# A planned attention-and-MLP kernel: load order, a third pair in halves, a new rule of choice in the planner, and one Gelu table load per phase

## The chip, the cores and the metric

The kernel runs on one core of a Trainium2 chip. The metric is the device time of one execution in microseconds, median of several runs. TensorE is called PE, VectorE DVE, ScalarE ACT, GpSimd POOL.

## The reference, cut to what matters

Inputs q, k, v and alpha are `(4, 8, 768, 48)`; the MLP is 384 -> 2048 -> 384.

```python
for t in range(S):                                     # gated linear attention, a state of 48 x 48 per head
    state = alpha[:, :, t, :, None] * state + einsum('bhd,bhe->bhde', k[:, :, t], v[:, :, t])
    y[:, :, t] = einsum('bhd,bhde->bhe', q[:, :, t], state)
x = y.transpose(0, 2, 1, 3).reshape(3072, 384)
h = x @ w_in
return gelu_tanh(h) @ w_out
```

## The kernel before

The 768 tokens are cut into 6 chunks of 128. A *unit* is one chunk of one batch, a *pair* is two units, and there are 12 pairs, 0 to 11. Each pair has a recurrent part (Ln of alpha, a cumulative sum as a matmul, exponentials, scaled q and k, their transposes, scores, mask, y, transposed x) and a *block* of MLP: layer 1 with 48 matmuls and 16 Gelus, layer 2 with 32 matmuls. Ln and Exp share one activation table, Gelu needs another, so ACT works in phases: the exponentials of the pair after next, then the Gelus of a block, then exponentials again.

The instruction order is not written by hand. A planner in the kernel knows every task with assumed durations and puts them in a fixed order. This is the choice that it makes for each engine:

```python
for t in left[e]:
    at = ready(t)
    if at is not None:
        found.append((max(at, free[e] + (W["table"] if t.table not in (None, table) else 0)), t))
if found:
    window = min(f[0] for f in found) + 60
    at, t = min((f for f in found if f[0] <= window), key=lambda f: (f[1].prio, f[0]))
```

`W["table"]` is 1290 ns. The copies (`x`, `ot`, and `ev` for the transposes of the first two pairs) can go to ACT or DVE and need no table. Other parts that matter:

```python
BUFS = dict(ca=1, yk=2, ff=4, ...)          # PSUM: "ca" single, for sums and scores; "ff" for hT and acc
LN_EXP, GELU = 6, 0
...
cum = s.add("cum", {"PE": W["cum"]}, P + 1, self.cum(u), [ln])        # P = 100 * pair; lower goes first
...
rows(0, 0, "qkv"); weights("in", (0, 1)); rows(0, 1); weights("in", (2, 3)); weights("out", range(4))
for c, i in pairs[2:]: rows(c, i)
...
for t in order:
    if t.load is not None:
        self.act_set(t.load)                # writes an ACT_TABLE_LOAD for Ln/Exp and for Gelu
    t.emit(t.engine)
```

## Time and profile before

| | before |
|---|---|
| median, four runs | 205.78 us (204.83 to 205.93) |
| profiled span | 204.1 us |
| PE busy / ACT busy / DVE busy | 185.2 / 151.0 / 105.6 us |
| table loads written / added at the Gelu | 20 / 10, each 1.283 us |
| mean granted clock of PE | 0.979 |

Busy time is a union over the span. The chain of the page follows the work that ended last backwards. A wait line reads "who waited, for whom: us in sum, times, longest". In a timeline, `[0.66 <-ACT gT L369]` is idle time just before the line and what ended it. In the names, `la` is Ln of alpha, `cum` its sum, `b`, `binv` and `bend` the exponentials, `qp` and `kp` the scaled q and k, `at` the scores, `yps` and `x` the result y and its copy, `hT` a layer-1 sum, `gT` its Gelu, `acc` and `ot` a layer-2 sum and its copy. The lines are in the prediction.

### The profile page before, as it was taken

What the parts mean: (1) busy time and instruction counts of PE and PEld (TensorE: products, weight loads), DVE (VectorE), ACT (ScalarE), POOL (GpSimd) and SP (SyncE); (2) the same over time, 40 slices, a digit from 0 to 9 for tenths busy, and PEclk for the clock granted to TensorE, in tenths of its full rate; (3) what the DMA queues carried; (4) which work ended last, traced back from release to release, by engine and by line L of the source; (5) the groups of instructions that cost most, each with busy time, mean ns of one, the idle gap of its engine ahead of it and who ended that gap; (6) DMA issues with size and microseconds to landing.
All of it is one profiled execution on the core that took longest, in us unless ns stands there. A gap on an engine that the chain in (4) does not pass through costs nothing.

```text
span 204.1 us, 4664 instructions
## 1 busy us (share of the span) xinstructions
PE 185.2 (91%) x1925; PEld 133.7 (65%) x1927; DVE 105.6 (52%) x219; ACT 151.0 (74%) x317; POOL 61.3 (30%) x63
## 2 busy tenths in 40 slices
PE   7786489999899989989989989989989989989992
PEld 2343358866578667767767767767777776676861
DVE  6373642037987394494494593594593550650000
ACT  2635767971789698798798798798798888883740
POOL 7983653464655664422410510000000000000000
PEclk9999958999999999999999999999999999999998
DMA  7999999999999999997980580200200200200202
GB/s 137 166 226 172 200 202 220 177 175 238 226 221 154 182 235 186 181 244 145 161 189 2 130 181 2 80 0 3 77 0 3 77 3 0 79 3 6 75 0 77
DMA packets 37941, 24.68 MB, mean 121 GB/s; under 512 B 27904, under 2 KB 34560, under 8 KB 37920
## 3 DMA queue, kind: packets, MB, share of 16 engines
q0 software_dynamic: 32400, 19.27, 67.2%
q1 hardware_dynamic: 5520, 5.11, 8.3%
q8 instruction: 15, 0.25, 0.6%
q14 instruction: 6, 0.05, 0.1%
HBM read 25.17 MB, written 4.72 MB: 146 GB/s over the span
## 4 chain that ended last, share of the span: by engine, by line
PE 70%; ACT 16%; DMA 6%; POOL 4%; issue 1%; DVE 1%; POOLq 0%; DVEq 0%
PE acc L377 31%; PE hT L363 27%; DMA k<-in_k_dram 6%; ACT L369 6%; ACT L181 6%; PE at L290 2%; PE yps L339 2%; ACT ot L384 2%; ACT gT L369 2%; PE cum L232 2%; PE yps L336 2%; PE xT_ps L353 2%; POOL q L202 1%; PE qkT_ps L268 1%; PE kv L307 1%
## 5 line engine op out<-in xcount | busy, mean ns | idle before, releaser
L363 PE MATMUL hT<-xT,w_in 128*128 128x256 bf16 x576 | 74.9, 278 | 8.1 <-ACT gT L369 7.9
L377 PE MATMUL acc<-w_out,gT 128*128 128x384 bf16 x384 | 68.4, 326 | 0.0
L369 ACT ACTIVATE gT<-hT 128x256 bf16<-128x256 f32 x192 | 62.0, 388 | 6.1 <-PE hT L363 5.6
L363 PEld LDWEIGHTS <-w_in 128*128 128x128 bf16 x576 | 54.6, 99 | 17.5 <-issue 9.4
L377 PEld LDWEIGHTS <-gT 128*128 128x128 bf16 x384 | 36.0, 98 | 20.4
L297 DVE TENSOR_TENSOR atm<-at,ut 128x512 bf16<-128x512 f32 x48 | 30.8, 684 | 8.1 <-PE at L290 7.0
L257 DVE TENSOR_TENSOR qp<-q,b 128x768 bf16<-128x768 f32 x12 | 11.5, 958 | 32.8 <-ACT b L249 32.8
L181 ACT ACT_TABLE_LOAD x20 | 25.7, 1283 | 1.1 <-PEq L576 0.7
L384 ACT COPY ot<-acc 128x384 f32<-128x384 f32 x18 | 8.6, 478 | 16.9 <-PE acc L377 16.7
L202 POOL DMA_DIRECT2D v<-in_v_dram x12 | 13.8, 1153 | 17.6 <-PE xT_ps L353 9.7
L346 ACT CAST x<-yps 128x384 bf16<-128x384 f32 x22 | 10.5, 478 | 11.5 <-PE yps L339 11.3
L202 POOL DMA_DIRECT2D a<-in_alpha_dram x11 | 12.7, 1153 | 20.7 <-ACT la L222 13.4
L278 DVE COPY qkT<-qkT_ps 128x1024 bf16<-128x1024 bf16 (+1 forms) x21 | 13.3, 673 | 7.6 <-PE qkT_ps L268 7.6
L357 DVE COPY xT<-xT_ps 128x384 bf16<-128x384 bf16 x24 | 8.5, 356 | 16.6 <-PE xT_ps L353 16.5
L202 POOL DMA_DIRECT2D q<-in_q_dram x12 | 14.0, 1163 | 9.9 <-DVE qp L257 4.2
L202 POOL DMA_DIRECT2D k<-in_k_dram x12 | 13.8, 1152 | 4.8 <-DVE stmp L322 2.3
L249 ACT ACTIVATE b<-cum 128x768 bf16<-128x768 f32 x12 | 9.7, 810 | 7.4 <-PE cum L234 7.4
L222 ACT ACTIVATE la<-a 128x768 f16<-128x768 f32 x12 | 10.1, 843 | 4.1 <-DMA a<-in_alpha_dram 4.0
L369 ACT ACT_TABLE_LOAD x10 | 12.8, 1283 | 0.1
L257 DVE TENSOR_TENSOR kp<-k,binv 128x768 bf16<-128x768 f32 (+1 forms) x14 | 11.6, 837 | 2.4 <-DMA k<-in_k_dram 2.4
L190 PE MATMUL idle<-zero 128*128 128x512 bf16 x37 | 11.3, 432 | 1.3 <-DVE zero L542 1.2
L324 DVE TENSOR_TENSOR st<-stmp,bend 64x192 bf16<-64x192 f32 x32 | 11.3, 353 | 1.7
(43 smaller groups left out, 167.2 us busy)
## 6 DMA issues: line engine op xcount, KB each, us to landing
q<-in_q_dram POOLq DMA_DIRECT2D x12, 384.0 KB, 12.6
k<-in_k_dram POOLq DMA_DIRECT2D x12, 384.0 KB, 12.7
out_dram<-ot SPq DMA_DIRECT2D x24, 192.0 KB, 1.9
a<-in_alpha_dram POOLq DMA_DIRECT2D x11, 384.0 KB, 12.6
v<-in_v_dram POOLq DMA_DIRECT2D x12, 192.0 KB, 12.6
w_in<-in_moe_w_in_dram POOLq DMA_DIRECT2D x4, 384.0 KB, 10.1
w_out<-in_moe_w_out_dram POOLq DMA_DIRECT2D x4, 384.0 KB, 14.7
a<-in_alpha_dram SPq DMA_DIRECT2D x1, 384.0 KB, 4.1
```

The lines of the kernel that those rows point to most:

```text
L181: nc.scalar.add_instruction(mybir.InstLoadActFuncSet(name=nc.get_next_instruction_name(), act_func_set_id=i, engine=mybir.EngineType.Activ ...
L190: self.nc.tensor.matmul(ps, self.zero[:, 0:self.C], self.zero, start=True, stop=True)
L202: (nc.sync if e == "SP" else nc.gpsimd).dma_start(t.rearrange("t b h d -> t (b h) d"), src)
L257: self.nc.vector.tensor_tensor(u[n + "p"][:, lo:hi, :, 0:self.D], u[n][:, lo:hi], u["b" if n == "q" else "binv"][:, lo:hi], op=ALU.mult)
L278: self.copy(e)(t, u.pop(("T_ps", i, which)))
L297: self.nc.vector.tensor_tensor(u["atm", i][:, o], u["at", i][:, o], self.ut[:, None, :].to_broadcast([self.C, self.H // 2, self.C]), op=AL ...
L324: nc.vector.tensor_tensor(new[ps, :, fs], acc, u["bend"][ps, i, :, None].to_broadcast([64, H // 2, D]), op=ALU.mult)
L346: self.copy(e)(x, u["y", i].rearrange("t h d -> t (h d)"))
L363: self.nc.tensor.matmul(h, self.w_in[:, j, nt * self.C:(nt + 1) * self.C], self.xT[c][:, j, lo:hi].rearrange("p g t -> p (g t)"), start=j ...
L369: return lambda e: self.nc.scalar.activation(self.gT[c % self.NG][:, nt, lo * self.C:hi * self.C], f.pop(("h", c, lo, nt)), AF.Gelu_apprx_ ...
L377: self.nc.tensor.matmul(f["acc", c, b], self.gT[c % self.NG][:, nt, b * self.C:(b + 1) * self.C], self.w_out[:, nt, :], start=nt == 0, sto ...
L384: self.copy(e)(f["ot", c, b], f.pop(("acc", c, b)))
```

## The change

Its intent: pairs 0 and 1 land first, then all weights, then the rest; pair 2 is loaded and scaled in halves; the cumulative sum is put ahead of other work; only the Ln/Exp table is loaded by hand. The diff also touches the planner's rule of choice and the idle matmuls that keep PE's clock up. Cut to its core:

```diff
+    SPLIT = (2,)
+    LOADS = ("0", "1", "in 0", "in 1", "in 2", "in 3", "out 0", "out 1", "out 2", "out 3", "2", "3", ...)
 ...
-                        found.append((max(at, free[e] + (W["table"] if t.table not in (None, table) else 0)), t))
+                        turn = W["table"] if t.table not in (None, table) else 0
+                        at = max(at, free[e] + turn)
+                        found.append((at, t, at - turn))
                 if found:
-                    window = min(f[0] for f in found) + 60
-                    at, t = min((f for f in found if f[0] <= window), key=lambda f: (f[1].prio, f[0]))
+                    window = min(f[2] for f in found) + 60
+                    at, t, _ = min((f for f in found if f[2] <= window), key=lambda f: (f[1].prio, f[0]))
 ...
                 n = int((at - max(free[e], ...) - 100) * 0.8 // W["fill"])
+                if not free[e]:
+                    n = int((at - W["zero"]) // W["cold"])
 ...
-            cum = s.add("cum", {"PE": W["cum"]}, P + 1, self.cum(u), [ln])
+            for lo, hi in self.parts(m):            # one part, or two where the pair is split
+                cum = s.add("cum", {"PE": W["cum"] * n // 2}, P - 400, self.cum(u, lo, hi), [ln])
 ...
-            if t.load is not None:
-                self.act_set(t.load)
+            if t.load == LN_EXP:
+                self.act_set(LN_EXP)
```

Cut: the bookkeeping for halves, a larger qkT tile, options that stay off (transposes by DMA), retuned durations, and a new order in layer 2 of block 0, which now takes each part of w_out for both units before the next part.

## The prediction

> **What bounds the kernel now.** I read the page first (busy shares, slices, chain), then the waits of PE, then the timeline in three places: one steady period, the start, and the passage to the third block. The work is 12 pairs of (chunk of 128 tokens, two batches), called pair 0 to 11. Each pair has a recurrent part and a block of layer 1 (48 matmuls and 16 Gelus, called L1) and layer 2 (32 matmuls, L2).
>
> ```profile
> PE 185.2 (91%) x1925; PEld 133.7 (65%) x1927; DVE 105.6 (52%) x219; ACT 151.0 (74%) x317; POOL 61.3 (30%) x63
> ...
> PE   7786489999899989989989989989989989989992
> ...
> PEclk9999958999999999999999999999999999999998
> DMA  7999999999999999997980580200200200200202
> ...
> PE 70%; ACT 16%; DMA 6%; POOL 4%; issue 1%; DVE 1%; POOLq 0%; DVEq 0%
> ```
>
> PE is busy 91% of the span and is 70% of the chain. Below 9 it dips in the first six slices, where the clock also drops to 5 tenths, and then once in every three slices. DMA is full until slice 18, about 92 us. So PE is the bound from about 57 us, and the start belongs to transfers and waits. All PE waits between 71 and 190 us, where PE is busy 113.05 of 118.9 us, are one group:
>
> ```profile
> PE hT L363 <- ACT gT L369: 5.8, 8, 0.9
> ```
>
> One period of the steady part shows what they are:
>
> ```profile
> 85.49 0.48 ACT L384 COPY ot<-acc 128x384 f32<-128x384 f32 x1 [0.39 <-PE acc L377]
> ...
> 85.98 1.28 ACT L181 ACT_TABLE_LOAD   x1
> ...
> 87.27 1.28 ACT L369 ACT_TABLE_LOAD   x1
> ...
> 88.57 2.50 ACT L369 ACTIVATE gT<-hT 128x256 bf16<-128x256 f32 x8
> 89.00 0.49 PE L363 MATMUL hT<-xT,w_in 128*128 128x256 bf16 x3 [0.66 <-ACT gT L369]
> ```
>
> Two table loads run back to back. The first (L181) is the one that the kernel writes; the second stands at the Gelu's own line and the kernel does not write it. PE has filled its four PSUM buffers of hT by then and stands 0.66 us for the first Gelu. The page counts 20 loads at L181 and 10 at L369: 10 for Ln/Exp, 10 written for Gelu, 10 more at the Gelu. The start shows the same pair of loads:
>
> ```profile
> 21.67 1.03 DVE L257 TENSOR_TENSOR kp<-k,binv 128x384 bf16<-128x384 f32 x2 [1.32 <-DMA k<-in_k_dram]
> 21.86 1.17 POOL L202 DMA_DIRECT2D a<-in_alpha_dram  x1 [1.81 <-DMA k<-in_k_dram]
> ...
> 23.33 1.28 ACT L181 ACT_TABLE_LOAD   x1
> ...
> 24.61 1.28 ACT L369 ACT_TABLE_LOAD   x1
> ...
> 26.34 0.80 PE L363 MATMUL hT<-xT,w_in 128*128 128x256 bf16 x3 [2.13 <-ACT gT L369]
> ```
>
> Here k of pair 1 lands at 21.67 us; its transposes are copied by ACT before the table is changed, so the first Gelu comes at 25.91. PE is empty from 24.4 to 26.34 and then has a clock of 0.57 until 32.8 (a window over that stretch). Blocks 0 and 1 end their L1 at 39.4. Last, the passage to block 2:
>
> ```profile
> 45.52 0.85 ACT L222 ACTIVATE la<-a 128x768 f16<-128x768 f32 x1
> ...
> 52.62 0.33 PE L232 MATMUL cum<-la,ut_h 128*128 128x384 f16 x1
> ...
> 57.89 0.66 ACT L369 ACTIVATE gT<-hT 128x256 bf16<-128x256 f32 x2
> ```
>
> The Ln of pair 3 is done at 46.4, but its cumulative sum waits to 52.62: the PSUM buffer "ca" is single, shared with the attention scores, and the two units of pair 2 are placed first. Gelu of block 2 needs the exponentials of pair 3, so it starts at 57.89, while L1 of block 2 starts at 57.14 behind 0.7 to 1 us of idle fill.
>
> **What the Trainium skill says.** "ScalarE: Activation LUTs", section "What ACT_TABLE_LOAD costs", gives about 1283 ns for a load plus a drain of about 1380. The trace agrees on 1283 and shows no drain here: 85.98, 87.27 and 88.57 follow one another with ACT already empty. The same page, "Table sets: the hidden batching unit", says that a compiler pass puts a load before every activation that needs one, and that the tanh-approximated Gelu is a set of its own. That fits a second load beside the written one; leaving out the written load should then be safe and cost nothing. "TensorE: Matmul & The Clock Gate", section "Part 1: The HAM clock gate", has half clock after an idle window of about 3.4 us. The trace shows about half clock (0.57), with 15 L1 matmuls in 3.20 us against 15 in 1.64 later; the empty stretch before was only 1.94 us, though there were others before it. "DMA: Bandwidth & Descriptors", section "Specifications", has rows under 512 B as slow. Agreed: a strip of q or k has rows of 192 B, and a 384 KB strip takes 2.35 us (q of pair 1 at 19.3, k at 21.67), a weight part of twice the bytes read about 1.9.
>
> **The change, part by part.** *Loads.* Bytes do not change, only their order: two weight parts pass behind pair 1. From the POOL waits (POOL waits for the transfer eight issues earlier) the landings before are: k of pair 0 9.3, second w_in part 15.05, alpha of pair 1 16.9, q 19.3, k 21.67, third and fourth w_in 24.7 and 26.4, w_out 28.4, 30.3, 32.4 and about 34.4, alpha of pair 2 36.45, alpha of pair 3 44.7. Moving 2 x 1.9 us of weights gives as estimates: alpha of pair 1 13.1, q 15.5, k 17.8, v 19.3; w_in 21.2, 23.1, 24.8, 26.4; w_out and pair 3 as before.
> Pair 1 then finishes its recurrent part near 24.5 instead of 33.5. L1 of block 0 starts with the first w_in at about 21.2 and is paced by the parts; its last four rows start at 26.4 and take 12 x 0.109 = 1.3 us, so it ends at 27.8. L1 of block 1 is 48 x 0.109 = 5.25 us, to 33.1. Before, that point was 39.4: 6.2 us gained, of which some 2.5 is the slow clock (30 matmuls at 0.21 instead of 0.109, less what lay beside), because PSUM is free for idle fill until 21.2.
>
> *Third pair unit by unit, cumulative sum first.* In halves, alpha of unit 0 lands near 35.5 and unit 1's k near 41.7. The "ca" buffer is free of pair 2's sums only after unit 1's exponentials, about 41.6. Attention of its units then takes the buffer to about 45.4 (twice a score group and 1.29 us of masks). Alpha of pair 3 lands at 44.7, Ln ends 45.5, its sum is now placed before other work, and its three exponentials end near 47.9; one table load gives a Gelu at about 49.2. PE has from 33.1 on: L2 of two blocks 64 x 0.163 = 10.4, pair 2's part 3.9 (the steady period's 14.37 busy less 5.25 and 5.21), pair 3's sum 0.5: to about 48.0. So L1 of block 2 starts effectively at 48.3 instead of 57.14: 8.8 us in all, including the 6.2.
>
> *One load per phase.* Ten loads of 1.283 us go, 12.8 us of ACT. PE gets back only its own waits: 5.8 us in eight phases. The first phase's share and block 2's are inside the 8.8. Layer 1, layer 2 and the tail after the last matmul (3.7 us) do not change. Splitting pair 2 adds some ten small instructions off the path.
>
> Sum: 204.1 - 8.8 - 5.8 = 189.5 us of span. I add 1.5 us for what a fixed order always loses against such arithmetic (parts of w_in that come late, PE waiting in order behind a half pair). That is 191.0; the timed runs lie 1.6 us over the profiled span (205.69 against 204.1), so 192.6, rounded to 192.5.
>
> **The rivals.** First: ACT stays the bound of the period. ACT's loop is Gelu start to last Gelu 5.9 us, then x copy, load, Ln, sum, exponentials, ot copy, two loads to the next Gelu start, about 9.1; that is 15.0, exactly the period. With one load it is 13.8, under PE's 14.37, so PE takes over with 0.6 us to spare. If other waits eat the margin, only part of the 5.8 comes: about 195. Second: the weights now come late, so the gain at the start is hidden: w_in at 23 and up instead of 21.2, or PE goes cold between parts and runs L1 of block 0 at 0.57. Then 3 to 4 us come back: about 196. But blocks 0 and 1 end under the same w_out landings, and pair 3's alpha at 44.7 bounds block 2 in any case, so such a loss is partly hidden. Third: transfers bind block 2 harder than I think, since half strips have twice the issues on POOL (1.15 us for a whole strip, perhaps 0.9 for a half, against a wire time of about 1.1) and only eight are in flight. If pair 3's alpha slips by 2 us, so does block 2: 194.5. Fourth: everything fits and the 1.5 is not lost: 191.0. Slower than before would need the new Gelu load to be missing or doubled, or a badly broken order; nothing in the profile speaks for it.
>
> **Range and chances.** The table-load term is read straight from waits, so about 5 us are nearly sure, which alone is over 2%. The start is worth 4 to 9. From 190.0 (all fits and a little more) to 197.5 (start gains half) should hold it 8 times in 10. Faster by over 2% 0.96, within 2% 0.03, slower 0.01.
>
> **What would show it.** Table loads: 10 at the written line and 10 at the Gelu's, ACT busy near 139. PE waits of hT for gT after 60 us: under 1 us in place of 5.8, and a period of Gelu starts of about 14.4 in place of 15.05. First Gelu at 21.5 to 23, no slices of low clock near 26 to 33 us, L2 of block 0 starting at 33 to 34, Gelu of block 2 at 49 to 50. If hT still waits for Gelu in each phase, the first rival holds; if the period falls and block 2 starts after 52, the start's sum was wrong. DMA should be as full as before to about 90 us, PE at about 95%.

## The result and the profile after

| | before | after |
|---|---|---|
| median, four runs each | 205.78 us | 192.81 us (192.75 to 192.87) |
| ratio of the fast runs, 95% interval | | 0.9379 (0.935 to 0.9407) |
| profiled span | 204.1 us | 191.0 us |
| period of Gelu starts, blocks 4 to 9 | 15.05 us | 14.15 us |
| hT of block 2 starts | 57.14 us | 50.51 us |
| hT of block 2 to the end of the span | 146.96 us | 140.49 us |
| PE / ACT / DVE busy | 185.2 / 151.0 / 105.6 | 181.4 / 135.8 / 111.2 us |

The two rows about block 2 add up to the span's difference: 6.63 us are won before its first hT and 6.47 us after, 13.1 us in all. The cut is not quite like for like: the 16 transposes of pair 3's q and k, some 0.9 us of PE, come before that hT in the kernel before (55.87 to 57.14) and after it in the changed kernel (51.49 to 52.38). These are the lines of the page after that answer to those in the prediction:

```profile
PE 181.4 (95%) x1919; PEld 131.8 (69%) x1922; DVE 111.2 (58%) x232; ACT 135.8 (71%) x300; POOL 63.8 (33%) x67
...
PE   5887899999999999999999999999999999999992
...
PEclk9999999999999999999999999999999999999999
DMA  6999999999999999999998770200200201101101
...
PE 75%; DMA 17%; POOL 4%; issue 1%; DVE 1%; ACT 1%; POOLq 0%; DVEq 0%
```

ACT has left the chain (16% to 1%), the dip of the clock is gone, and from the sixth slice to the last but one PE is never below 9 tenths. A window from 60 to 176 us has PE busy for 116.00 of 116.00 us, and the list of PE's waits in it is empty. ACT has lost 15.2 us: 12.8 for ten table loads, and some copies that went to DVE (x on ACT 22 to 14, ot 18 to 16), less what the Gelus (62.0 to 64.5 us of busy time) and the halves add. DVE has gained 5.6.

Those moved copies are the first sign of something that the prediction did not count. One period of ACT in the kernel before:

```profile
92.84 1.65 ACT L369 ACTIVATE gT<-hT 128x256 bf16<-128x256 f32 x5
95.18 0.48 ACT L346 CAST x<-yps 128x384 bf16<-128x384 f32 x1 [0.69 <-PE yps L339]
95.68 1.28 ACT L181 ACT_TABLE_LOAD   x1
...
99.97 0.18 ACT L245 ACTIVATE bend<-cum 128x8 f32<-128x8 f32 x1
100.54 0.48 ACT L384 COPY ot<-acc 128x384 f32<-128x384 f32 x1 [0.39 <-PE acc L377]
101.04 1.28 ACT L181 ACT_TABLE_LOAD   x1
```

and in the kernel after:

```profile
85.14 1.98 ACT L404 ACTIVATE gT<-hT 128x256 bf16<-128x256 f32 x6
87.14 1.28 ACT L198 ACT_TABLE_LOAD   x1
88.43 0.84 ACT L241 ACTIVATE la<-a 128x768 f16<-128x768 f32 x1
90.05 0.48 ACT L419 COPY ot<-acc 128x384 f32<-128x384 f32 x1 [0.77 <-PE acc L412]
...
91.95 0.18 ACT L266 ACTIVATE bend<-cum 128x8 f32<-128x8 f32 x1
92.15 1.28 ACT L404 ACT_TABLE_LOAD   x1
```

Before, ACT had done its last Gelu at 94.49, then stood for PE, copied x, and only then loaded the table at 95.68; after the exponentials it stood again, copied ot and loaded at 101.04 in place of 100.15. That is 1.19 + 0.89 = 2.08 us of ACT's loop per period, spent ahead of the two table changes. After, both loads come at once, and the ot copy runs at 90.05, where ACT stands for the sum in any case (0.75 us at 98.57 before). The old rule explains it: a task that needs another table counts as ready 1290 ns later, so any copy that becomes ready within that time, with higher priority or not, is taken first, and ACT waits idle for it. The new rule compares tasks without the table's time.

At the start, in the kernel before, ACT waited 0.80 us for a copy of k's transposes, made it in 0.58, and only then loaded the table at 23.33. After, pair 1 lands earlier, ACT is done with its copies of the transposes by 21.53, and the table comes next. That is the order of loads; what the rule does at the start, `b_rule` below shows. After:

```profile
21.55 1.28 ACT L404 ACT_TABLE_LOAD   x1
...
21.77 1.47 PE L398 MATMUL hT<-xT,w_in 128*128 128x256 bf16 x12
```

and the passage to block 2:

```profile
33.60 2.76 PE L412 MATMUL acc<-w_out,gT 128*128 128x384 bf16 x16
...
47.67 0.33 PE L252 MATMUL cum<-la,ut_h 128*128 128x384 f16 x1
...
50.51 1.14 PE L398 MATMUL hT<-xT,w_in 128*128 128x256 bf16 x9
...
51.27 0.94 ACT L404 ACTIVATE gT<-hT 128x256 bf16<-128x256 f32 x3
```

Layer 2 of block 0 starts at 33.60 (before 39.22), but block 2 starts 2.2 us after the 48.3 that I had worked out.

### The profile page after: what moved, and what is told of

The parts are those of the page before. It is cut to its first block, busy times and chain, and to the rows that moved or that the text cites. A ratio compares the mean times of both kernels' runs of the same rounds, so it can differ in the third digit from the quotient of the medians.

```text
span 191.0 us, 4655 instructions
## 1 busy us (share of the span) xinstructions
PE 181.4 (95%) x1919; PEld 131.8 (69%) x1922; DVE 111.2 (58%) x232; ACT 135.8 (71%) x300; POOL 63.8 (33%) x67
## 4 chain that ended last, share of the span: by engine, by line
PE 75%; DMA 17%; POOL 4%; issue 1%; DVE 1%; ACT 1%; POOLq 0%; DVEq 0%
PE acc L412 29%; PE hT L398 28%; DMA k<-in_k_dram 9%; DMA w_out<-in_moe_w_out_dram 8%; PE qkT_ps L289 5%; PE at L325 3%; PE yps L374 2%; PE yps L371 2%; PE kv L342 2%; PE xT_ps L388 2%; PE cum L252 2%; POOL q L220 1%; PE cum L254 1%; POOL a L220 1%; POOL k L220 1%
## 5 line engine op out<-in xcount | busy, mean ns | idle before, releaser
L404 ACT ACTIVATE gT<-hT 128x256 bf16<-128x256 f32 x192 | 64.5, 385 | 16.3 <-PE hT L398 15.6
L398 PE MATMUL hT<-xT,w_in 128*128 128x256 bf16 x576 | 71.6, 273 | 0.1
L398 PEld LDWEIGHTS <-w_in 128*128 128x128 bf16 x576 | 53.6, 98 | 8.1 <-issue 0.4
L278 DVE TENSOR_TENSOR qp<-q,b 128x768 bf16<-128x768 f32 (+1 forms) x13 | 11.6, 896 | 33.2 <-ACT b L270 33.2
L419 ACT COPY ot<-acc 128x384 f32<-128x384 f32 x16 | 7.7, 478 | 19.0 <-PE acc L412 19.0
L220 POOL DMA_DIRECT2D a<-in_alpha_dram x12 | 13.3, 1110 | 15.3 <-ACT la L241 8.8
L220 POOL DMA_DIRECT2D v<-in_v_dram x13 | 14.4, 1111 | 8.0 <-PE hT L398 1.9
L303 DVE COPY qkT<-qkT_ps 128x1024 bf16<-128x1024 bf16 (+1 forms) x22 | 13.8, 663 | 5.5 <-PE qkT_ps L289 5.5
L220 POOL DMA_DIRECT2D k<-in_k_dram x13 | 14.5, 1113 | 7.3 <-DVE xT L392 2.0
L198 ACT ACT_TABLE_LOAD x10 | 12.8, 1283 | 0.9 <-PEq L627 0.7
L241 ACT ACTIVATE la<-a 128x768 f16<-128x768 f32 (+1 forms) x13 | 10.3, 794 | 3.9 <-DMA a<-in_alpha_dram 3.7
L404 ACT ACT_TABLE_LOAD x10 | 12.8, 1283 | 0.2
L270 ACT ACTIVATE b<-cum 128x768 bf16<-128x768 f32 (+1 forms) x13 | 9.9, 762 | 4.1 <-PE cum L254 3.7
L359 DVE TENSOR_TENSOR st<-stmp,bend 64x192 bf16<-64x192 f32 x32 | 11.3, 353 | 2.1 <-ACT gT L404 0.5
L357 DVE TENSOR_TENSOR stmp<-kv,st 64x192 f32<-64x192 f32 x32 | 11.2, 351 | 0.2
## 6 DMA issues: line engine op xcount, KB each, us to landing
q<-in_q_dram POOLq DMA_DIRECT2D x11, 384.0 KB, 13.1
w_in<-in_moe_w_in_dram POOLq DMA_DIRECT2D x4, 384.0 KB, 11.8
w_out<-in_moe_w_out_dram POOLq DMA_DIRECT2D x4, 384.0 KB, 15.2
```

Of the source, the lines that this page charges most:

```text
L198: nc.scalar.add_instruction(mybir.InstLoadActFuncSet(name=nc.get_next_instruction_name(), act_func_set_id=i, engine=mybir.EngineType.Activ ...
L220: (nc.sync if e == "SP" else nc.gpsimd).dma_start(u[n][:, lo:hi].rearrange("t b h d -> t (b h) d"), src)
L241: self.nc.scalar.activation(u["la"][:, lo:hi, :, 0:self.D], u["a"][:, lo:hi], AF.Ln)
L278: self.nc.vector.tensor_tensor(u[n + "p"][:, lo:hi, :, 0:self.D], u[n][:, lo:hi], u["b" if n == "q" else "binv"][:, lo:hi], op=ALU.mult)
L303: self.copy(e)(t, u.pop(("T_ps", i, which)))
L357: nc.vector.tensor_tensor(s[ps], acc, old[ps, :, fs], op=ALU.add)
```

## The experiments

Three theories. **A**: the written Gelu load is what PE waits for in each phase, and leaving it out gives the steady part's gain. **B**: the new order of instructions gives it. **C**, formed after the first four runs: the rule of choice is that part of the new order, and rule and load hide the same waits. Beside them, what the order of loads, the halves, the early sum and the idle matmuls are worth at the start.

All twelve gave correct results.

| run | what | median us | ratio to before, 95% interval |
|---|---|---|---|
| changed kernel | | 192.81 | 0.9379 (0.935 to 0.9407) |
| b_one_load | before, one Gelu load | 197.16 | 0.9619 (0.9586 to 0.9653) |
| a_two_loads | after, second load back | 193.39 | 0.9434 (0.9398 to 0.9471) |
| b_new_order | before, new load order | 202.64 | 0.9883 (0.9844 to 0.9922) |
| a_old_order | after, old load order | 193.71 | 0.9440 (0.9409 to 0.9472) |
| b_rule | before, new rule, two loads | 195.89 | 0.9568 (0.9513 to 0.9622) |
| a_old_rule | after, old rule | 204.56 | 0.9969 (0.9933 to 1.0004) |
| a_old_rule_two | after, old rule, two loads | 215.87 | 1.0523 (1.0483 to 1.0562) |
| a_cum_late | after, old priority of the sum | 191.95 | 0.9352 (0.9318 to 0.9386) |
| b_rule_one | before, new rule, one load | 194.60 | 0.9484 (0.9436 to 0.9532) |
| a_whole_third | after, third pair whole | 194.90 | 0.9488 (0.9456 to 0.9521) |
| a_no_fill | after, no idle matmuls | 193.98 | 0.9450 (0.9417 to 0.9484) |
| a_late_warm | a_cum_late and a longer first fill | 191.96 | 0.9344 (0.9317 to 0.9371) |

The median of the kernel before was 205.05 to 205.78 us in the four sets of rounds. Differences under about 1 us between rows are read with that in mind.

### b_one_load and a_two_loads: the load by itself

```diff
 b_one_load, on the kernel before
-            if t.load is not None:
-                self.act_set(t.load)
+            if t.load == LN_EXP:
+                self.act_set(LN_EXP)
 a_two_loads, on the changed kernel: the reverse
```

> The kernel before with only the written Gelu load left out; its order of instructions is unchanged. Theory A (the second load is what PE waits for in each phase): the 5.8 us of PE waits between 71 and 190 us fall under 1 us, the period goes from 15.05 to about 14.3 us, the first Gelu comes 1.3 us earlier; 197.5 to 199 us in all, so 7 to 8 us off. Theory B (the gain of the steady part comes from the new order of instructions, in which the Gelu's first sums lie elsewhere): less than 3 us off, over 203 us.

> The changed kernel with the written Gelu load put back, order unchanged. Theory A: PE waits come back in each phase, period about 15.0, 198.5 to 200 us. Theory B (the new order leaves ACT 2 us of waits for PE in each period, so that a second load is hidden there): 193 to 195 us, PE waits under 2 us in sum. A mixture would lie between.

Measured: taking the load out of the kernel before gives 8.1 us (205.28 to 197.16), and its period falls to 14.23 us. Putting it back into the changed kernel costs only 0.6 us, and the period stays at 14.15. PE's waits for the Gelu over the whole span, in b_one_load:

```profile
PE hT L363 <- ACT gT L369: 0.3, 1, 0.3
```

and in a_two_loads:

```profile
PE hT L398 <- ACT gT L404: 1.1, 2, 0.7
```

So A is right for the kernel before and B for the changed kernel. In the kernel before, leaving out the load is enough to remove the waits (197.16 us is a little under A's range), but in the changed kernel it is not needed for it: the changed kernel has something else that hides a second load.

### b_new_order and a_old_order: the order of loads

```diff
 b_new_order, on the kernel before
-        weights("in", (0, 1))
         rows(0, 1)
+        weights("in", (0, 1))
         weights("in", (2, 3))
 a_old_order, on the changed kernel
-    LOADS = ("0", "1", "in 0", "in 1", "in 2", ...)
+    LOADS = ("0", "in 0", "in 1", "1", "in 2", ...)
```

> The kernel before with only the order of loads changed (two pairs, all weights, the rest), planned again by its own scheduler. If the order of loads gives the gain of the start by itself: layer 2 of block 0 starts at 34 to 36 us in place of 39.2, layer 1 of block 2 about 4 us earlier, 200 to 202.5 us, steady period still 15.05. Rival (the start is bound by pair 3 and the single PSUM buffer, so that it needs the third pair's halves and the earlier sum too): layer 2 starts earlier but layer 1 of block 2 stays near 57, 204 to 206 us.

> The changed kernel with only the old order of loads. If the order of loads carries the start: the first Gelu near 25, layer 1 of block 2 at 53 to 55 us in place of 50.5, 195.5 to 198 us. Rival (pair 3's arrival bounds block 2 whatever lies before): layer 1 of block 2 within 1 us of 50.5, 192.5 to 194 us.

Alone, the new order gives 2.6 us: layer 2 of block 0 starts at 34.39 in place of 39.22, but half of these 4.8 us are lost by block 2, whose hT starts at 54.83 (before 57.14). That is a little outside my range and between the two theories. In the changed kernel the old order costs 0.9 us: hT of block 2 starts 2.3 us later (52.78), and part of it is caught up within two blocks (the Gelu of block 4 starts at 80.28 against 79.35). The time is the rival's; the start of block 2 lies between the two, and the first Gelu, at 21.61, is not near 25, since the new rule puts the table before a copy of k (21.89).

### b_rule, a_old_rule, a_old_rule_two: the rule of choice

```diff
 b_rule, on the kernel before: the lines of the rule as in the change's diff, nothing else
 a_old_rule, on the changed kernel: the same lines taken back
 a_old_rule_two: a_old_rule, and the written Gelu load back
```

> The kernel before with only the planner's rule of choice changed: a task is no longer held back in the choice by the table load that it needs. Both loads at each Gelu phase stay. Theory C (the rule is what makes room: the Ln table is loaded right after the last Gelu, the copy of the second unit's x goes to DVE, so ACT's loop no longer waits twice for PE): period about 14.2 to 14.4 us with two loads, PE waits for the Gelu under 2 us, 198 to 200.5 us. Theory A (only a load taken out gives the gain): period stays near 15.0, 204 to 206 us.

> The changed kernel with the old rule of choice, one load per phase. Theory C together with the run of one load: either remedy alone is enough, so the period stays at 14.15 to 14.3 us and the time within 1.5 us of the changed kernel, 192.5 to 194.5 us. If the rule also serves the start, layer 1 of block 2 comes later and it is 195 us or more.

> The changed kernel with the old rule and with the written Gelu load: both remedies taken away, load order, halves and early sum kept. If the two remedies are the whole of the steady part's gain, the period returns to 15.0 us and the time is 198.5 to 201 us. If something else in the new order gives it, it stays under 196 us.

The rule alone, with both loads left in, gives 9.2 us (205.05 to 195.89), the most of any single part by the median (its interval and that of the load alone overlap), and 2.1 us below the range that I had given. PE waits for a Gelu once between 71 and 176 us, 0.5 us. Its timeline in the steady part, with both loads:

```profile
79.65 0.18 ACT L247 ACTIVATE bend<-cum 128x8 f32<-128x8 f32 x1
79.85 1.28 ACT L183 ACT_TABLE_LOAD   x1
...
81.14 1.28 ACT L371 ACT_TABLE_LOAD   x1
...
82.44 0.94 ACT L371 ACTIVATE gT<-hT 128x256 bf16<-128x256 f32 x3
...
83.86 1.37 ACT L371 ACTIVATE gT<-hT 128x256 bf16<-128x256 f32 x4 [0.48 <-PE hT L365]
```

Now ACT waits for PE, not PE for ACT. The arithmetic closes, as an estimate: ACT's loop of 15.05 us less the 2.08 us in front of the table changes is 12.97 us, under PE's 14.15, so a second load fits. Less one load instead it is 13.77 us, under PE too. In this plan, either remedy takes ACT off the path. With the old load order the rule also serves the start: its first Gelu is at 22.72 in place of 25.91, since ACT no longer makes copies of the transposes before the load (it makes one after, at 23.00; DVE makes the other three), and a window from 26 to 33 us has a granted clock of 1.00 where the kernel before had 0.57 to 32.8.

Here is the miss: I expected the changed kernel under the old rule to lose next to nothing, because one load should be enough. It lost 11.8 us and is within 2% of the kernel before. None of that is lost at the start: hT of block 2 comes at 50.29, against 50.51 with the new rule. Its period is 15.86 us:

```profile
91.64 0.48 ACT L379 CAST x<-yps 128x384 bf16<-128x384 f32 x1 [1.33 <-PE yps L372]
93.23 0.48 ACT L417 COPY ot<-acc 128x384 f32<-128x384 f32 x1 [1.10 <-PE acc L410]
93.72 1.28 ACT L196 ACT_TABLE_LOAD   x1
```

In this plan two copies, not one, are taken ahead of the load, since after each copy the 1290 ns are counted anew, so 3.4 us pass between the last Gelu (90.31) and the load. All that follows is late, and the wait appears in another place: PE has no wait for a Gelu between 71 and 176 us, but it waits for the products of the late exponentials:

```profile
PE qkT_ps L287 <- DVE qp L276: 5.4, 6, 0.9
PE qkT_ps L287 <- DVE kp L276: 2.8, 6, 0.5
```

With the second load on top (a_old_rule_two) it is another 11.3 us for ten loads of 1.283, which is what a load costs where ACT is the bound. My range for it, 198.5 to 201 us, took the plan for that of the kernel before and was missed by 15 us. Why the old rule hurts this plan more than the plan before, which parts of the change bring the second copy into the window, was not separated and stays open.

### b_rule_one: do rule and load add up?

```diff
 b_rule, and the written Gelu load left out
```

> The kernel before with the new rule of choice and one Gelu load per phase; load order, whole third pair and late sum as before. Theory C (rule and load hide the same waits, so that the second adds little to the first): 194.3 to 195.7 us, so 0.2 to 1.6 us under the rule alone at 195.9. If the two gains were separate and added up, it would be near 188 us.

194.60 us, 1.3 us under the rule alone, within the range: they do not add up. Load 8.1 and rule 9.2 give 10.7 together (205.35 to 194.60). All other parts of the change, together, are worth the remaining 1.8 us to 192.81, when they come last.

The profiles show where. From hT of block 2 to the end of the span, the kernel before takes 146.96 us, with the load left out 140.24, with the new rule 140.24, with both 139.67: after block 2 each remedy gives the same 6.7 us, and both hardly more. Block 2 itself starts at 57.14, 55.16, 53.26 and 52.63.

### a_cum_late and a_whole_third: the sum and the halves

```diff
 a_cum_late:     cum = s.add("cum", ..., P - 400, ...)  ->  P + 1
 a_whole_third:  SPLIT = (2,)  ->  ()
```

> The changed kernel with the old priority of the cumulative sum. If placing the sum before other work carries the start of block 2: sum of pair 3 later than 47.7 us, layer 1 of block 2 at 52 us or later, 194 to 196 us. Rival (only few instructions move, and pair 2's own units bound the block): within 0.7 us of the changed kernel.

> The changed kernel with the third pair whole. If the halves carry the start of block 2 as I predicted: layer 1 of block 2 at 51.5 to 53 us in place of 50.5 and 194 to 195.5 us. Rival (PE has layer 2 of two blocks to do meanwhile, so that the pair is hidden either way): within 0.7 us of the changed kernel at 192.8.

Placing the sum first does not help, it costs: with the old priority the median is 191.95, 0.9 us less, and the profiled span is 189.9 against 191.0. The ratio's intervals overlap, so the size is uncertain; that it would be a gain of 1 to 3 us is refuted. The sum of pair 3 starts at 47.50 there, no later than with the early priority (47.67), but behind unit 1's last y, so its xT and the hT of block 2 come at 49.08 in place of 50.51. The halves, by contrast, are worth 2.1 us (194.90 without). In that run the early sum of pair 3 takes the single "ca" buffer at 45.36, the scores of pair 2's second unit wait until 48.46, and hT of block 2 starts at 53.75 (I had said 51.5 to 53). So the two interact through the one buffer; what the halves are worth with the late sum was not run.

### a_no_fill and a_late_warm: the idle matmuls

```diff
 a_no_fill:    Scheduler(self.BUFS, self.fill, 60000)  ->  Scheduler(self.BUFS, None, 60000)
 a_late_warm:  a_cum_late, and in the first burst
-                    n = int((at - W["zero"]) // W["cold"])
+                    n = 13
```

> The changed kernel without the idle matmuls that fill PE's gaps at the start. If the clock of the first 30 us matters as predicted (some 2.5 us in the kernel before): granted clock near 0.5 to 0.6 where layer 1 of block 0 begins, layer 2 of block 0 at 35 to 36 us in place of 33.5, 194 to 196 us. Rival (transfers pace the start, and fills themselves delay pair 0): 192.3 to 193.3 us.

> A version meant to beat both: the changed kernel with the old priority of the cumulative sum and 13 idle matmuls in the first burst, as before the change, in place of 6. In the changed kernel the short first burst leaves PE cold, so that the second burst of 7 takes 3.15 us and holds the first transposes from about 8.6 to 9.5 us. If that delay is on the path: first hT near 20.8 in place of 21.7 and 190.8 to 191.5 us. If transfers or later waits take it up: 191.7 to 192.2 us, as with the old priority alone.

Without fills it is 193.98, 1.2 us more, the lower edge of what I expected: PE is cold in the whole recurrent part of the first two pairs (the 8 transposes of pair 1's q take 1.03 us in place of 0.65), layer 1 of block 0 starts 1.1 us later, its first group is still cold (12 matmuls in 2.04 us in place of 1.47), and layer 2 starts at 35.23, within my 35 to 36. The longer first burst brings first hT to 21.12 in place of 21.68, yet the time is 191.96, the same as a_cum_late. Layer 2 starts 0.55 us earlier (32.95), and hT of block 2 still starts at 49.23 against 49.08: what is won is lost again by the arrival of pair 2 and by the order in its passage. So the rival holds. Both versions are faster than the changed kernel by medians (191.95 and 191.96 against 192.81); no version here beats it clearly by the ratio's interval.

## Why the prediction was right or wrong

**The time**: 192.5 predicted, 192.81 measured. That it came out so close is in part luck: the terms erred in opposite directions, and the 1.5 us that were added took up the rest.

**Loads and start**: first Gelu at 22.84 (said 21.5 to 23), layer 2 at 33.60 (said 33 to 34), clock without the dip: right. But hT of block 2 gained 6.6 us, not 8.8, and its Gelu came at 51.27 (said 49 to 50). The step that was off is "its sum is now placed before other work": the sum ran at 47.67 and not at 45.5, because the second unit's scores held "ca" and stood behind a group of layer 2 on PE; and the early priority delayed unit 1's y, where I had counted it as a help.

**What the gain at the start comes from**: right in kind, too large in size, and wrong in sign for the sum. The prediction gave the 8.8 us to the order of loads, the halves and the sum, with one load less in the first phases. `a_old_rule_two` has these parts with the old rule and both loads: its hT of block 2 starts at 51.31, 5.8 us earlier than before. One load less brings it to 50.29 (`a_old_rule`), and the rule adds nothing to that. But the parts are not the only way: in the kernel before, the rule alone brings hT of block 2 to 53.26. So undone one at a time they look small: the order 0.9 us, the halves 2.1, the sum about -0.9.

**A misreading**: the prediction has PE empty from 24.4 to 26.34, 1.94 us. That was the edge of a window; PE's last instruction before it ends at 24.21, and the line shown there says 2.13.

**One load per phase**: "PE gets back only its own waits: 5.8 us in eight phases" is right as a size. The waits went to zero and the part after block 2 gained 6.5 us; 0.7 more than the waits. Two things of that size stand against each other: layer 1's own busy time per period fell by 0.16 us (6.22 before, 88.57 to 103.62; 6.06 after, 79.35 to 93.50), some 1.3 us in eight, and the 0.9 us of transposes moved behind the cut. As a cause it is half right: it is what the load gives in the kernel before (8.1 us with the start), but in the changed kernel the load is worth 0.6. And it would not have been enough there: one load with the old rule has a period of 15.86 us.

**The step that failed** is the list of parts itself. The first rival counted "x copy, load, Ln, sum, exponentials, ot copy" as a fixed loop of ACT. The diff's new rule takes both copies out of the front of the loads, and the prediction gave it no term. It is worth 9.2 us alone and 11.8 in the changed kernel, against 0.6, 8.1 or 11.3 for the load, by what it stands beside. The prediction also took ACT's loop with one load, 13.8 us, from the old plan; the new plan under the old rule needs 15.86. The result was met because rule and load remove the same wait, which could be counted once only, and because the rule, not counted, was in the change: without it the same prediction would have met 204.56.

**The 1.5 us for an imperfect order**: the shortfall at block 2 was 2.2 us and the steady part's surplus 0.7; so 1.5 in sum, by cancellation rather than by insight.

**The 14.4 us period**: 14.15. PE's busy time in the old trace, 14.37, still held that 0.16 us of layer 1, so it was not its floor; the other 0.06 was not traced.

## What to carry to other kernels

When two changes remove the same wait, each can seem to be worth the whole of it when tried alone and nearly nothing when undone at the end; only the 2 x 2 of runs (both, either, none) shows it. When a fixed order is made by a planner, read a change of its choosing rule as a change of the schedule, and look in the old trace for what stands directly in front of an expensive mode change: there an engine pays for the small copy and for the wait that leads to it. Before giving a resource "first" to some task, ask who else needs its single buffer.

## What the Trainium skill lacked or had wrong

- "ScalarE: Activation LUTs", section "What ACT_TABLE_LOAD costs", budgets about 2.66 us for a switch, with the drain. In these traces a switch behind finished work is 1.283 us and the next Gelu follows at once (loads at 85.98 and 87.27, Gelu at 88.57). The page does not say that a load written by hand for the Gelu may be followed by the compiler's own; here that doubled it, ten times 1.283 us. The written load for Ln/Exp is not followed by a second one; why the Gelu's is was not tested, and a wrong set number in `GELU = 0` is not excluded.
- The same section has no word on what a load costs a kernel. Here ten loads cost 0.6, 8.1 or 11.3 us, by whether ACT was off the path, near it, or the bound.
- "TensorE: Matmul & The Clock Gate", section "Part 1: The HAM clock gate", asks for an idle window of about 3.4 us. The kernel before had a granted clock of 0.57 after an empty stretch of 2.13 us, with shorter ones before it. The page's caveat that the clock's events can be unreliable is borne out: in the changed kernel the granted clock reads 1.00 in the first 10 us, while 7 idle matmuls took 3.15 us there and 1.67 us in a_late_warm.
- No page treats the order of copies around a table change, which was worth 9.2 us alone here.
